# Two more key blocks per head on VectorE, one piece of the output projection loaded otherwise, and fewer semaphore waits, in a one-token attention and MLP kernel

## The chip, the cores and the metric

The kernel runs on one core of a Trainium2 chip. The metric is device time in microseconds (us). The kernel before takes 198.02 us, the median of three runs (198.01 to 198.27). Engine names are those of the profile: PE is TensorE, PEld its weight loads, DVE is VectorE, ACT is ScalarE, POOL is GpSimd, SP is SyncE (which here only issues DMAs).

## The reference

One token `x` (512 numbers) goes through an attention block with a cache of 4096 keys and values for each of 32 heads, and through an MLP; a gate mixes both.

```
g = sigmoid(sum(x * gate_w))
q = (x @ wq) as 32 heads of 128                       # wq: 512 x 4096
scores = q . k * 128**-0.5 ;  p = softmax(scores)     # k: 32 x 4096 x 128
o = p @ v                                             # v: 32 x 4096 x 128
a = o.reshape(4096) @ wo                              # wo: 4096 x 512
b = relu(x @ w1 + b1)**2 @ w2 + b2                    # w1: 512 x 1376, w2: 1376 x 512
out = g * a + (1 - g) * b
```

All tensors are bf16. Keys and values are 1 MB per head each, so 64 MB of the 78.76 MB that the kernel moves; wq and wo are 4 MB each.

## The kernel before

**Loads.** SP's queue first issues wq in four parts, then for each head one load of the keys (`load_k`) and one of the values (`load_v`), the keys seven heads ahead (`LAG = 7`). Each of keys and values has a ring of eight buffers. `load_k(h)` waits until head `h - 8` has been scored and transposed (`s_sd`, `s_t`), `load_v(h)` until the product with the values of head `h - 8` is done (`s_pv`). w1 is inserted at head 8. The last loads behind the last head's values are, in order: 8 of wo's 32 row groups (heads 24 to 31, `wob_sb`, into key buffer 0), eight tenths of w2 (`w2a`), the 128 rows of wo of head 23 (`wox`, into key buffer 1), the last 96 rows of w2 (`w2b`), and the last two tenths of w2.

**Pieces of wo.** The rows of wo of heads 0 to 22 are loaded as 92 pieces. A piece is 32 rows, 32 KB, and goes to one partition of tile `W`, over the space of wq, when all queries have been computed. The lists `RUNS` and `FIRST` (lines 59 to 65) say which partitions the pieces go to: an entry names a kind of place, a DMA engine `e`, and a number of pieces `k`, for engines `e`, `e + 1` and so on. `RUNS` are 14 DMAs from POOL's queue (lines 307 to 320), with 9 small DMAs between them that only advance the position from which engines are dealt out; `FIRST` are 5 DMAs that SP issues at heads 20 to 24 (lines 275 to 278). POOL then builds a selection matrix with one instruction for each of the 19 entries (lines 330 to 335).

**Scores.** A head has 32 blocks of 128 keys. The first `XB = 16` are scored on VectorE: `ttr(h)` does one multiply-and-sum instruction for each block against a broadcast query, in place on the key tile (line 629). The other `YB = 16` are transposed on TensorE in two halves (`transposes`, line 427), copied from PSUM by ScalarE (`evac`, line 361) and multiplied with the query column (`scores`, line 438). `smax(h)` on VectorE copies TensorE's scores beside its own and takes a maximum per partition (lines 635, 638). Every four heads (`G = 4`) share one maximum: `max_rows`, `gmax`, `max_cols`; ScalarE then computes the four exponentials (`exps`), and `pv(h)` on TensorE multiplies with the values (line 463).

**Order.** Every engine runs a hand-written loop over `i` from 0 to 38. At step `i` VectorE does `ttr(i)`, then `smax(i - 1)`; TensorE does `transposes(i)`, `scores(i - 1)`, and `pv(i - 7)` at the end of the step. At `i = 24` TensorE has the first MLP layer (`mlp_h`); at `i = 25` VectorE follows with `mlp` (lines 661 to 671) and POOL with a memset and its selection matrices.

**The end.** After `ttr(31)` VectorE normalises heads 16 to 23 (`norm(2)`, line 656). TensorE turns the result (`turn_a`, `spread_a`), VectorE copies it (lines 699 to 704), waits for all pieces of wo, and multiplies nine of the 32 row groups of the loaded pieces itself in `part_y` (lines 676, 679; `TD = 23`). TensorE does the other 23 in `out_a`, and adds VectorE's sum in `sum_y` (line 537), which stands ahead of `pv(30)` and `pv(31)` in its order. Then come `norm(3)`, `regroup`, `out_b` (line 525, heads 24 to 31), `mlp_out(0)`, `out_x` (line 531, head 23), `mlp_out(1)`, `mlp_out(2)` (line 546), the final add and transpose on VectorE (lines 717, 719), and the store.

## Time and profile before

| what | value |
|---|---|
| median of 3 runs | 198.02 us (198.01 to 198.27) |
| the profiled execution | 198.08 us, of which the span from first to last instruction is 196.3 us |
| DMA | 78.76 MB, mean 401 GB/s |
| PE busy | 132.9 us (68%) |
| PEld busy | 118.8 us (61%) |
| DVE busy | 139.5 us (71%) |
| ACT busy | 79.5 us (41%) |
| POOL busy | 29.9 us (15%) |

The 1.78 us between the profiled execution's time and its span lie around the span. In a group of instructions, the first number after the bar is the time in which at least one of them ran, then the mean of one in ns, then the idle time of the engine just before them and what ended it. In a table by stretches, each engine has its busy time and, in brackets, how many instructions ran; behind them stand the clock granted to TensorE, the share in which the DMA engines were busy, and what they moved in GB/s. In a timeline, a row is a run of equal instructions: start, length, engine, line, operation, tiles, count, and in square brackets the idle time before it and who ended it.

### The profile page before, as it was taken

Reading aid. Unit: us, or ns where it says so; the run is one execution under the profiler, and the core shown is the slowest. Engines: PE = TensorE matmul, PEld = TensorE weight load, DVE = VectorE, ACT = ScalarE, POOL = GpSimd, SP = SyncE. Lnnn points to the kernel's source line nnn. Section 1 sums busy time; section 2 is a strip of 40 time slices with the busy share of each in tenths; the row PEclk is TensorE's granted clock in tenths of the full one; section 3 lists DMA queues with packets and bytes.
Section 4 is the critical chain, followed back from the end, with each engine's and each line's share of the span. In section 5 each row is a group of like instructions: output and inputs, shape, how many; then the busy total and the mean of one; then the engine's idle time right before and its main releaser. Section 6 shows DMA issues by size and latency. Waiting matters only on the chain.

```text
span 196.3 us, 6564 instructions
## 1 busy us (share of the span) xinstructions
PE 132.9 (68%) x2402; PEld 118.8 (61%) x2408; DVE 139.5 (71%) x1152; ACT 79.5 (41%) x148; POOL 29.9 (15%) x53
## 2 busy tenths in 40 slices
PE   0128756699876867806697760769998677785872
PEld 0105725578675667706676760668997666785862
DVE  0307999999998687707877871777779999949310
ACT  2105838356473536503356330633077334611000
POOL 2000000000000000000019940000099750000000
PEclk9999978555585555665555555555555555555555
DMA  6999999999999999999999999999999999999990
GB/s 226 425 427 426 416 416 426 419 422 416 411 422 422 412 417 407 423 421 417 421 416 421 416 414 409 409 409 414 413 416 416 426 412 422 419 417 414 416 351 28
DMA packets 12730, 78.76 MB, mean 401 GB/s; under 512 B 2502, under 2 KB 2728, under 8 KB 3369
## 3 DMA queue, kind: packets, MB, share of 16 engines
q1 hardware_dynamic: 11146, 75.77, 93.6%
q0 software_dynamic: 1536, 2.56, 3.5%
q8 instruction: 19, 0.31, 0.6%
q14 instruction: 15, 0.11, 0.2%
q10 hardware_dynamic: 14, 0.01, 0.0%
HBM read 78.32 MB, written 0.00 MB: 399 GB/s over the span
## 4 chain that ended last, share of the span: by engine, by line
DMA 59%; DVE 22%; PE 9%; SPq 6%; issue 3%; ACT 0%
DMA Kt<-in_A_k_cache_dram 42%; DVE Kt L629 18%; DMA w2a<-in_B_w_dram 12%; DMA W<-in_A_wq_dram 6%; SPq L265 4%; PE KP L427 3%; PE pX L481 2%; DVE S L629 1%; SPq L260 1%; PE pQ L405 1%; PE pX L477 1%; PE pX L546 1%; SPq L254 1%; PE pS L438 1%; DVE dg L644 0%
## 5 line engine op out<-in xcount | busy, mean ns | idle before, releaser
L629 DVE CUSTOM_DVE_ANT_0 Kt<-Kt,qb 128x128 bf16<-128x128 bf16 x512 | 113.3, 289 | 23.2 <-DMA Kt<-in_A_k_cache_dram 23.2
L361 ACT ACTIVATE kT<-KP 128x1024 bf16<-128x1024 bf16 x64 | 61.8, 1021 | 68.8 <-PE KP L427 68.8
L427 PE MATMUL KP<-ident,Kt 128*128 128x128 bf16 x512 | 56.8, 300 | 32.8 <-DMA Kt<-in_A_k_cache_dram 32.8
L427 PEld LDWEIGHTS KP<-ident,Kt 128*128 128x128 bf16 x512 | 49.5, 140 | 35.6 <-DMA Kt<-in_A_k_cache_dram 34.4
L629 DVE DVE_READ_ACCUMULATOR2_ANT S<- 128x1 f32 x512 | 41.0, 80 | 0.0
L438 PEld LDWEIGHTS pS<-qcol,kT 128*128 128x128 bf16 x512 | 18.5, 107 | 10.7 <-DVE S L635 10.5
L438 PE MATMUL pS<-qcol,kT 128*128 128x1 bf16 x512 | 19.1, 167 | 8.4 <-DVE S L635 8.2
L315 POOL DMA_DIRECT2D xb<-in_B_w_dram x9 | 5.3, 590 | 100.3 <-PE pQ L405 100.3
L405 PE MATMUL pQ<-W,xb 128*128 128x512 bf16 x26 | 12.4, 620 | 7.8 <-DMA W<-in_A_wq_dram 6.4
L463 PEld LDWEIGHTS pO<-E,Vt 128*128 128x128 bf16 x512 | 15.5, 104 | 1.1 <-issue 0.8
L463 PE MATMUL pO<-E,Vt 128*128 128x1 bf16 x512 | 16.1, 165 | 0.0
L333 POOL TENSOR_SCALAR_AFFINE_SELECT w_sb<-w_sb 24x36 bf16<-24x36 bf16 (+5 forms) x19 | 11.0, 578 | 2.7
L353 ACT ACTIVATE qb<-pQ 128x512 bf16<-128x512 f32 x8 | 4.7, 591 | 14.9 <-PE pQ L405 14.9
L405 PEld LDWEIGHTS pQ<-W,xb 128*128 128x128 bf16 x32 | 3.6, 130 | 10.8 <-issue 10.8
L372 ACT ACTIVATE E<-S,nM 128x32 bf16<-128x32 f32 x32 | 9.9, 309 | 0.3
L463 PE MATMUL pQ<-E,Vt 128*128 128x1 bf16 x256 | 8.1, 165 | 2.3 <-DMA Vt<-in_A_v_cache_dram 2.0
L463 PEld LDWEIGHTS pQ<-E,Vt 128*128 128x128 bf16 x256 | 7.7, 104 | 2.5 <-issue 2.4
L463 PEld LDWEIGHTS pX<-E,Vt 128*128 128x128 bf16 x256 | 7.7, 103 | 0.5 <-issue 0.2
L463 PE MATMUL pX<-E,Vt 128*128 128x1 bf16 x256 | 8.0, 165 | 0.0
L318 POOL DMA_DIRECT2D W<-in_A_wo_dram x14 | 7.8, 563 | 0.0
L615 DVE CAST qcol<-pQ 128x4 bf16<-128x4 f32 x8 | 1.2, 152 | 8.4 <-PE pQ L413 8.4
L635 DVE COPY S<-pS 128x16 f32<-128x16 f32 x32 | 5.4, 168 | 2.2 <-PE pS L438 2.2
(84 smaller groups left out, 93.0 us busy)
## 6 DMA issues: line engine op xcount, KB each, us to landing
Kt<-in_A_k_cache_dram SPq DMA_DIRECT2D x32, 1024.0 KB, 27.2
Vt<-in_A_v_cache_dram SPq DMA_DIRECT2D x32, 1024.0 KB, 27.2
W<-in_A_wq_dram SPq DMA_DIRECT2D x4, 1024.0 KB, 7.9
W<-in_A_wo_dram POOLq DMA_DIRECT2D x2, 768.0 KB, 12.8
w_sb<-in_B_w_dram SPq DMA_DIRECT2D x4, 344.0 KB, 22.9
Kt<-in_A_wo_dram SPq DMA_DIRECT2D x1, 1024.0 KB, 21.5
w2a<-in_B_w_dram SPq DMA_DIRECT2D x1, 1024.0 KB, 23.3
W<-in_A_wo_dram POOLq DMA_DIRECT2D x10, 64.0 KB, 23.5
```

What stands on the lines that cost most here:

```text
L265: eng.dma_start(Vt[:, h % NV, :], v_h[h, :, :]).then_inc(s_v[h % NV], 16)
L315: eng.dma_start(dm[0:d, sent, :, 0:8], src[:, :, 0:8]).then_inc(s_dm[sent], 16)
L318: eng.dma_start(W[p:p + st * (k - 1) + 1:st, :], woa_v[q:q + k, :], max_dma_last_dim=8192).then_inc(s_wp[n], 16)
L333: eng.affine_select(out=part, in_=part, compare_op=ALU.not_equal, fill=1.0, base=-st * q, pattern=[[st, 4], [-1, st * (k - 1) + 1]], chann ...
L361: eng.activation(kT[:, h % 2, j * HB * 128:(j + 1) * HB * 128], KP[n % 3][:, :], ACT.Copy).then_inc(s_ev, 1)
L372: eng.activation(E[:, h % NE, :], S[:, h % NS, :], ACT.Exp, bias=nM[:, h:h + 1], scale=SCALE, accum_out=RS[:, h:h + 1]).then_inc(s_e, 1)
L405: mm = eng.matmul(pQ[:, :], xb[:, t, :], wq_sb[:, t, c * 512:(c + 1) * 512], start=(t == 0), stop=(t == 3))
L427: mm = eng.transpose(KP[n % 3][:, y * 128:(y + 1) * 128], Kt[:, h % NK, b * 128:(b + 1) * 128], ident[:, :])
L438: mm = eng.matmul(S2[:, y:y + 1], kT[:, h % 2, y * 128:(y + 1) * 128], qcol[:, h:h + 1], start=True, stop=True)
L463: mm = eng.matmul(O(h, h + 1), Vt[:, h % NV, b * 128:(b + 1) * 128], E[:, h % NE, b:b + 1], start=(b == 0), stop=(b == NB - 1))
L629: ins = eng.tensor_tensor_reduce(kb, kb, qb[:, h * 128:(h + 1) * 128], 1.0, 0.0, ALU.mult, ALU.add, S[:, h % NS, b:b + 1])
L635: eng.tensor_copy(S[:, h % NS, XB:NB], S2).then_inc(s_cp, 1)
```

## The change

- `XB` is 18: VectorE scores 18 of 32 blocks per head, TensorE transposes and multiplies 14 (two halves of 7).
- `RUNS` loses the entry with engines 3 and 4 (two pieces, POOL's queue). The last entry of `FIRST` has three pieces instead of two, on engines 0, 1 and 2. Pieces per engine, engines 0 to 15: before 8 7 6 1 6 5 5 8 8 5 5 5 5 5 5 8, after 8 7 7 0 5 5 5 8 8 5 5 5 5 5 5 8. 91 pieces are left.
- The 32 rows of the piece that fell out (the first 32 dimensions of head 22) are loaded as 32 rows of 1 KB into partitions 0 to 31 (`woy`), with one more DMA from SP behind `wox`; `out_x` has four more matmuls for them, and waits for both loads. The piece's number (`QX`) is skipped in the selection matrix.
- The pieces of POOL's queue count on one semaphore instead of 14, so TensorE and VectorE wait once where they had 14 waits each.
- Waits are left out or joined: `transposes` waits for ScalarE only in its second half from the third half on; `scores` waits for the query column and `ttr` for the broadcast query only at every fourth head; `pv` and `ttr` wait for the exponentials once for a group of four (for the group's last) instead of at every head.

```
-    XB = 16
+    XB = 18
...
-            (SEAM, 7, 2, 1, 1), (WRAP, 15, 2, 1, 1), (OUTER, 1, 2, 1, 1), (OUTER, 3, 2, 1, 1),
+            (SEAM, 7, 2, 1, 1), (WRAP, 15, 2, 1, 1), (OUTER, 1, 2, 1, 1),
...
-             (OUTER, 0, 2, 0, 1)]
+             (OUTER, 0, 3, 0, 1)]
+    QX = 4 * (NA - 2)
...
         for run in RUNS + FIRST:
+            q += q == QX
             yield (*place(*run), q)
...
+        woy = Kt[0:32, 1, DM:2 * DM]
...
-        s_wp = [sem(f"s_wp{n}") for n in range(len(RUNS))]
+        s_wp = sem("s_wp")
...
             eng.dma_start(wox, A_wo[HX * 128:NA * 128, :]).then_inc(s_wx, 16)
+            eng.dma_start(woy, A_wo[32 * QX:32 * QX + 32, :]).then_inc(s_wx, 16)
...
-                    if n >= 3:
+                    if n >= 3 and j == 1:
                         eng.wait_ge(s_ev, n - 2)
...
-                eng.wait_ge(s_qc, h // 4 + 1)
+                if h % 4 == 0:
+                    eng.wait_ge(s_qc, h // 4 + 1)
...
             def pv(h):
-                eng.wait_ge(s_e, h + 1)
+                if h % G == 0:
+                    eng.wait_ge(s_e, h + G)
...
                     eng.wait_ge(s_ac, 2)
-                    for q in s_wp:
-                        eng.wait_ge(q, 16)
+                    eng.wait_ge(s_wp, 16 * len(RUNS))
...
             def out_x():
-                eng.wait_ge(s_wx, 16)
-                for j in range(4):
-                    eng.matmul(acc[:, j:j + 1], wox[:, j * 128:(j + 1) * 128], onorm[:, HX:HX + 1],
-                               start=False, stop=False, skip_group_check=True)
+                eng.wait_ge(s_wx, 32)
+                for w, o in ((wox, onorm[:, HX:HX + 1]), (woy, onorm[0:32, HX - 1:HX])):
+                    for j in range(4):
+                        eng.matmul(acc[:, j:j + 1], w[:, j * 128:(j + 1) * 128], o,
+                                   start=False, stop=False, skip_group_check=True)
...
                 eng.wait_ge(s_k[h % NK], 16 * (h // NK + 1))
-                eng.wait_ge(s_qb, h // 4 + 1)
-                if h >= NS:
-                    eng.wait_ge(s_e, h - NS + 1)
+                if h % 4 == 0:
+                    eng.wait_ge(s_qb, h // 4 + 1)
+                if h >= NS and h % G == 0:
+                    eng.wait_ge(s_e, h - NS + G)
...
                     eng.tensor_copy(o2D, O2A[:, TD:32]).then_inc(s_y2, 1)
-                    for q in s_wp:
-                        eng.wait_ge(q, 16)
+                    eng.wait_ge(s_wp, 16 * len(RUNS))
                     eng.wait_ge(s_wr, 16 * len(FIRST))
                     eng.wait_ge(s_y2, 1)
                     part_y()
```

More of the change, by code (lines that the diff above doesn't have):

```diff
@@ L318, in _ @@
                 eng.dma_start(W[p:p + st * (k - 1) + 1:st, :], woa_v[q:q + k, :],
-                              max_dma_last_dim=8192).then_inc(s_wp[n], 16)
+                              max_dma_last_dim=8192).then_inc(s_wp, 16)
                 q += k
-            assert q == STRIPS[len(RUNS)][3] and STRIPS[-1][3] + STRIPS[-1][2] == 4 * HX
+            assert q == STRIPS[len(RUNS)][3] and STRIPS[-1][3] == QX + 1 and STRIPS[-1][2] == 3
             for n in range(sent):
```

## The prediction

> **What bounds the kernel now.** First the page's slices: the loads run at their full rate from the second slice to the last but two.

> ```profile
> DMA  6999999999999999999999999999999999999990
> GB/s 226 425 427 426 416 416 426 419 422 416 411 422 422 412 417 407 423 421 417 421 416 421 416 414 409 409 409 414 413 416 416 426 412 422 419 417 414 416 351 28
> PEclk9999978555585555665555555555555555555555
> ```

> So time can be won only where the loads end, and lost where work after the last landing grows. The chain of waits, cut to the end, shows who closes the kernel.

> ```profile
> 168.74 23.26 DMA w2a<-in_B_w_dram
> ...
> 192.14 0.99 PE pX L546 x32
> 193.13 0.11 PE pX L531 x4
> 193.23 0.35 PE pX L546 x12
> ```

> A load does. Next the timelines of TensorE and VectorE, to see how far behind the load the other claimants stand.

> ```profile
> 172.28 0.22 DVE L656 SCALAR_TENSOR_TENSOR onorm<-pO,gcol,rden 128x8 bf16<-128x8 f32 x1
> 176.37 0.49 DVE L676 TENSOR_SCALAR kT<-W,S 128x512 f32<-128x512 bf16 x1 [0.85 <-DVE S L704]
> 176.89 6.26 DVE L679 SCALAR_TENSOR_TENSOR kT<-W,S,kT 128x512 f32<-128x512 bf16 x8
> 183.21 1.01 PE L537 MATMUL pX<-onesf,kT 128*128 128x1 f32 x4 [0.43 <-DVE kT L679]
> 186.96 0.99 PE L463 MATMUL pQ<-E,Vt 128*128 128x1 bf16 x32
> 190.63 0.69 PE L525 MATMUL pX<-o2B,Kt 128*128 128x1 bf16 x20 [0.38 <-issue]
> 192.14 0.99 PE L546 MATMUL pX<-hs,w2a 128*128 128x1 bf16 x32 [0.82 <-DMA w2a<-in_B_w_dram]
> ```

> This is a second chain, only 0.82 us shorter: VectorE ends part_y at 183.15, TensorE waits for it, then runs from 183.21 without a gap to pv(31), and on through norm, regroup and out_b to 191.32. Last, where VectorE has room: stretches that each begin with ttr(26), (27), ... (31).

> ```profile
> 147.19:150.93 3.74, 2.96 (x53) 2.61 (x53) 3.71 (x35) 2.78 (x12) 3.65 (x1) 0.50 1.02 418
> 150.93:155.77 4.84, 3.33 (x69) 2.98 (x68) 4.81 (x36) 1.82 (x3) 3.57 (x9) 0.50 1.02 425
> 155.77:160.70 4.93, 3.82 (x73) 3.47 (x72) 4.90 (x36) 1.92 (x4) 3.64 (x10) 0.50 1.00 410
> 160.70:164.82 4.12, 2.71 (x60) 2.62 (x58) 4.05 (x38) 1.08 (x3) 0.13 (x1) 0.50 1.02 422
> 164.82:168.57 3.75, 2.54 (x57) 2.43 (x56) 3.72 (x35) 3.21 (x11) 0.00 (x0) 0.50 1.03 422
> 168.57:172.28 3.71, 3.17 (x66) 3.09 (x67) 3.68 (x35) 1.94 (x2) 0.00 (x0) 0.50 1.00 417
> ```

> The third busy time is VectorE's: in 25.09 us it is idle 0.24. Whatever is added to these six heads arrives whole at part_y.

> **VectorE's two blocks.** ttr(26) starts at 147.19 and its 16 blocks end with the copy at 150.59: 3.40 / 16 = 0.2125 us per block, 0.425 per head. Heads 0 to 25: 26 x 0.425 = 11.1 us, hidden, because VectorE sat 23.2 us waiting for keys (the group of line 629). Its first idle is at 62 us, so until then key buffers come free up to about 13 x 0.425 = 5.5 us later; a load takes 27.2 us (median) from issue to landing, nearly all of it in the queue, so SP may be that late. Without this cover it would cost one to one. Heads 26 to 31 have no cover: 6 x 0.425 = +2.55.

> Heads 27 and 28 took 4.84 and 4.93 instead of 3.74 while POOL ran its selection instructions. If each added block is stretched like its neighbours, 4 x 1.1 / 16 = +0.27; if the stall belongs to POOL's instructions, of which there is one less (18 of 19; 2.2 / 19), -0.1. I take -0.1, since the first of these heads, beside one long POOL instruction, took 3.74 like the heads without POOL: the stall goes with the count of instructions. [...]

> **TensorE's and ScalarE's relief.** Two of 16 transposes (1.89 / 16 each) and of 16 score matmuls (0.42 / 16) fewer: 0.24 + 0.05 per head. Mostly this lies in TensorE's waits for keys (32.8 us) and ScalarE's for TensorE (68.8), so nothing. It counts once: from the keys of head 24 at 132.91 TensorE runs without a gap through mlp_h to 141.35; POOL's memset (142.31) and its first selection (145.11) start from that, and hold VectorE until 147.19. Up to mlp_h that is one head's transposes and scores: -0.26 (bounds 0, if POOL's start doesn't follow, and -0.55, if the second head's counted too).

> **Waits.** Before part_y VectorE passes 16 waits in the 0.85 us shown above; 3 stay. Other dependent pairs on VectorE stand 0.04 apart (168.39 to 168.43), so 0.81 can go at most; 13/16 is 0.69. I take -0.70 (bounds -0.5, -0.81). TensorE's 13 lie behind a matmul (175.06 to 175.62): nothing. The waits joined by fours: pv(28) waits for its group's last exponential, 177.1 before and 178.6 to 179.3 then, and started at 178.63; pv(29) waits for its values until 181.78, which hides it. ttr and scores wait for results some 8 heads old: nothing.

> **Pieces and loads.** Bytes are equal. POOL's queue has one 0.55 us issue less (13; the 9 small ones stay, with 45 rows for 43) and nobody waits for its end. SP issues woy in about 0.45, ahead of w2b and w2a's tail, which land 22.8 and 21.5 us after issue: hidden. The third FIRST piece adds nothing to SP. In out_x 4 matmuls more: +0.11 by the chain. Which engine ends last changes: 32 KB at 26.1 GB/s (418 / 16) is 1.26 us on one engine. TensorE's program shrinks by some 340 instructions, so the 0.38 "issue" gap may sit elsewhere: +/-0.38.

> **Sum.** part_y ends 2.55 - 0.10 - 0.26 - 0.70 = 1.49 us later; TensorE's gapless run carries that to out_b, 191.32 + 1.49 = 192.81. The load's 0.82 is covered first: 1.49 - 0.82 + 0.11 = +0.78. The w2a tail (193.20) is then no longer waited for. 198.08 + 0.78 = 198.86; the profiled execution lies 0.06 above the median, so against that 198.80.

> **Rivals.**
> (a) Faster: the load still closes the kernel, and ends earlier. These stretches show it running out of engines:

> ```profile
> 191.00:191.50 0.50, 0.32 (x12) 0.23 (x9) 0.00 (x0) 0.00 (x0) 0.00 (x0) 0.50 0.41 148
> 191.50:192.00 0.50, 0.00 (x0) 0.00 (x0) 0.00 (x0) 0.00 (x0) 0.00 (x0) 0.50 0.36 131
> 192.00:192.50 0.50, 0.36 (x14) 0.39 (x15) 0.00 (x0) 0.00 (x0) 0.00 (x0) 0.50 0.19 72
> 192.50:193.00 0.50, 0.50 (x25) 0.50 (x23) 0.00 (x0) 0.00 (x0) 0.00 (x0) 0.50 0.02 8
> ```

> Shares times 16: six engines after 191.5, three after 192, none after about 192.7. If the last two are engines 3 and 4, each with a piece less, the end moves to the next ones, about 192.25: -0.45, 197.6. It decides only if VectorE's delay stays below about 0.35 instead of 1.49, for instance if the keys of head 24 come a us earlier; their arrivals were 4.93 to 5.60 apart, so they do wander. Against it: six heads without idle time.
> (b) No change: delay and slack cancel (delay near 0.8) and the loads end where they did: 198.0.
> (c) Slower through the loads: engine 2's extra piece, 1.26, makes it last: 199.3. Against: only a share of 0.41 is busy at 191.0 to 191.5, so 9 engines could take a piece unseen. [...]

> **Chances.** My forecast 0.63, (c) 0.07, (a) 0.18, (b) 0.12. Its own range is 198.1 (gap gone, keys earlier) to 199.6 (stretched blocks +0.37, relief absent +0.26). With the others, 197.5 to 199.7 leaves out two in ten. The measurement tells about 0.2% (0.4 us) from no change: slower 0.68 (most of the forecast, and (c)), the same 0.14, faster 0.18.

> **What would show it.** Right: ttr heads in 147 to 175 at 4.17 without POOL; part_y starting less than 0.3 after its copy and ending near 184.6; the idle time before mlp_out(0) gone, out_b's end near 192.8. Wrong: part_y ending before 184.0, or TensorE still waiting for w2a at the end.

## The result, and the profile after

The changed kernel takes 199.3 us (median of 12 runs, 198.4 to 199.5), the kernel before 198.09 us (12 runs on the same chips, 198.0 to 198.35). The ratio is 1.0054, with a 95% interval of 1.0045 to 1.0063: slower by about 1.1 us. The forecast was 198.8 (197.5 to 199.7). The profiled execution took 199.33 us with a span of 197.5, against 198.08 and 196.3.

The page's slices of the changed kernel, what the DMA engines moved in each:

```profile
GB/s 226 426 427 427 418 417 422 417 425 417 420 415 417 422 418 403 422 422 425 413 422 415 417 415 410 414 407 410 418 418 417 420 420 415 420 422 420 414 261 4
```

The loads run as before, and the slice that was half filled holds less (261 GB/s in the last but one, 351 before; a slice is 4.9 us): the work behind the loads has grown. The chain of waits of the changed kernel, its last part, start and length of each step:

```profile
174.32 0.53 PE pS L443 x14
...
184.55 1.01 PE pX L543 x4
...
191.28 1.01 PE pX L530 x32
192.56 0.73 issue
193.29 0.75 PE pX L552 x22
194.34 0.43 PE pX L552 x12
```

The load of `w2a`, which closed the kernel before, is gone from the chain. In its place stand a copy of VectorE's that TensorE waits for (174.32), `sum_y` (184.55), `out_b` (191.28), and 0.73 us in which TensorE has nothing to wait for and doesn't run. The timelines of VectorE and of TensorE show the same steps (start, length, engine, line, operation, tiles, count, idle time before and its end):

```profile
174.40 0.22 DVE L663 SCALAR_TENSOR_TENSOR onorm<-pO,gcol,rden 128x8 bf16<-128x8 f32 x1
177.71 0.49 DVE L683 TENSOR_SCALAR kT<-W,S 128x512 f32<-128x512 bf16 x1
```

```profile
174.32 0.53 PE L443 MATMUL pS<-qcol,kT 128*128 128x1 bf16 x14 [2.74 <-DVE S L642]
180.45 0.51 PE L512 MATMUL pX<-o2A,W 128*128 128x1 bf16 x14 [0.93 <-issue]
184.55 1.01 PE L543 MATMUL pX<-onesf,kT 128*128 128x1 f32 x4 [1.45 <-DVE kT L686]
191.28 1.01 PE L530 MATMUL pX<-o2B,Kt 128*128 128x1 bf16 x32 [0.26 <-DVE o2B L720]
192.16 0.41 PE L552 MATMUL pX<-hs,w2a 128*128 128x1 bf16 x10
193.29 0.75 PE L552 MATMUL pX<-hs,w2a 128*128 128x1 bf16 x22 [0.73 <-issue]
193.90 0.44 PE L537 MATMUL pX<-onorm,Kt 128*128 128x1 bf16 x8
```

VectorE's `norm(2)` comes at 174.40 (before 172.28), the wait ahead of `part_y` is gone, and `sum_y` starts at 184.55 (183.21). The "issue" gap in `out_b` is gone too; a larger one lies in `mlp_out(0)`, and another at 180.45, ahead of a wait that hides it. Last, the stretches between VectorE's copies of TensorE's scores (from the start of `ttr(26)` to the copy, then from copy to copy; columns as in the prediction):

```profile
146.69:150.51 3.82, 2.09 (x30) 1.74 (x27) 3.82 (x38) 2.29 (x10) 3.75 (x1) 0.50 1.01 412
150.51:156.37 5.86, 3.06 (x60) 2.72 (x60) 5.83 (x39) 2.28 (x3) 4.50 (x10) 0.50 1.02 425
156.37:161.22 4.85, 3.33 (x62) 3.07 (x62) 4.82 (x39) 1.73 (x2) 2.94 (x8) 0.50 1.00 412
161.22:165.42 4.20, 3.30 (x61) 2.90 (x61) 4.17 (x42) 1.18 (x2) 0.00 (x0) 0.50 1.02 423
165.42:169.98 4.56, 3.73 (x62) 3.28 (x62) 4.49 (x41) 2.83 (x11) 0.00 (x0) 0.50 1.01 417
169.98:174.09 4.11, 1.39 (x46) 1.30 (x46) 4.08 (x39) 0.94 (x2) 0.00 (x0) 0.50 1.01 421
```

Cut at the same events the kernel before has 3.40, 4.83, 4.87, 3.77, 4.16 and 3.76. VectorE is still never idle (0.21 of 27.40 us), and the six stretches are 2.61 us longer together, the three without GpSimd 0.43, 0.40 and 0.35.

### The profile page after: what moved, and what is told of

Its sections match the earlier page's. It is cut to its first block, busy times and chain, and to the rows that moved or that the text cites. A ratio compares the mean times of both kernels' runs of the same rounds, so it can differ in the third digit from the quotient of the medians.

```text
span 197.5 us, 6356 instructions
## 1 busy us (share of the span) xinstructions
PE 128.5 (65%) x2284; PEld 111.3 (56%) x2284; DVE 152.7 (77%) x1280; ACT 72.9 (37%) x148; POOL 29.7 (15%) x51
## 4 chain that ended last, share of the span: by engine, by line
DVE 46%; DMA 32%; PE 14%; SPq 4%; issue 2%; ACT 0%; DVEq 0%
DVE Kt L636 35%; DMA Kt<-in_A_k_cache_dram 27%; DMA W<-in_A_wq_dram 6%; DVE kT L686 3%; DVE S L636 2%; SPq L268 2%; PE pX L487 2%; PE pQ L409 2%; PE pQ L469 2%; PE KP L431 2%; DVE mp L645 1%; DVE hs L673 1%; SPq L263 1%; PE pX L543 1%; DVE S L642 1%
## 5 line engine op out<-in xcount | busy, mean ns | idle before, releaser
L636 DVE CUSTOM_DVE_ANT_0 Kt<-Kt,qb 128x128 bf16<-128x128 bf16 x576 | 127.0, 288 | 14.3 <-DMA Kt<-in_A_k_cache_dram 14.3
L365 ACT ACTIVATE kT<-KP 128x896 bf16<-128x896 bf16 x64 | 55.1, 914 | 69.6 <-PE KP L431 69.6
L431 PE MATMUL KP<-ident,Kt 128*128 128x128 bf16 x448 | 51.5, 304 | 26.9 <-DMA Kt<-in_A_k_cache_dram 26.8
L431 PEld LDWEIGHTS KP<-ident,Kt 128*128 128x128 bf16 x448 | 44.2, 142 | 29.3 <-DMA Kt<-in_A_k_cache_dram 28.1
L636 DVE DVE_READ_ACCUMULATOR2_ANT S<- 128x1 f32 x576 | 45.7, 79 | 0.0
L443 PE MATMUL pS<-qcol,kT 128*128 128x1 bf16 x448 | 17.3, 167 | 21.8 <-DVE S L642 21.8
L443 PEld LDWEIGHTS pS<-qcol,kT 128*128 128x128 bf16 x448 | 16.2, 107 | 25.8 <-DVE S L642 25.8
L409 PE MATMUL pQ<-W,xb 128*128 128x512 bf16 x32 | 15.0, 623 | 6.2 <-DMA W<-in_A_wq_dram 6.2
L322 POOL DMA_DIRECT2D W<-in_A_wo_dram x13 | 7.3, 565 | 0.0
L645 DVE TENSOR_REDUCE mp<-S 128x1 f32<-128x32 f32 x32 | 5.9, 185 | 1.1
## 6 DMA issues: line engine op xcount, KB each, us to landing
w_sb<-in_B_w_dram SPq DMA_DIRECT2D x4, 344.0 KB, 22.8
w2a<-in_B_w_dram SPq DMA_DIRECT2D x1, 1024.0 KB, 22.8
```

The source lines that it names most:

```text
L322: eng.dma_start(W[p:p + st * (k - 1) + 1:st, :], woa_v[q:q + k, :], max_dma_last_dim=8192).then_inc(s_wp, 16)
L365: eng.activation(kT[:, h % 2, j * HB * 128:(j + 1) * HB * 128], KP[n % 3][:, :], ACT.Copy).then_inc(s_ev, 1)
L409: mm = eng.matmul(pQ[:, :], xb[:, t, :], wq_sb[:, t, c * 512:(c + 1) * 512], start=(t == 0), stop=(t == 3))
L431: mm = eng.transpose(KP[n % 3][:, y * 128:(y + 1) * 128], Kt[:, h % NK, b * 128:(b + 1) * 128], ident[:, :])
L443: mm = eng.matmul(S2[:, y:y + 1], kT[:, h % 2, y * 128:(y + 1) * 128], qcol[:, h:h + 1], start=True, stop=True)
L636: ins = eng.tensor_tensor_reduce(kb, kb, qb[:, h * 128:(h + 1) * 128], 1.0, 0.0, ALU.mult, ALU.add, S[:, h % NS, b:b + 1])
```

## The experiments

Three theories stood against each other. Theory 1: VectorE's two blocks, late at `part_y`. Rival 1: the pieces, that is, the loads. Rival 2: TensorE's "issue" gaps, that is, the supply of its instructions. Ratios are against runs of the kernel before on the same chip, with 95% intervals; "gap" is idle time of TensorE that the profile calls "issue".

| run | median us | ratio |
|---|---|---|
| e1, blocks only | 200.04 | 1.0093 (1.0078 to 1.0108) |
| e2, all but the blocks | 198.24 | 1.0005 (0.9995 to 1.0014) |
| e3, pieces only | 198.18 | 1.0005 (0.9996 to 1.0014) |
| e4, waits only | 197.87 | 0.9984 (0.9974 to 0.9993) |
| e5, six row groups on VectorE | 199.68 | 1.0068 (1.0049 to 1.0087) |
| e6, 384 waits in front | 198.45 | 1.0016 (1.0006 to 1.0025) |
| e7, 13 waits before `part_y` | 199.27 | 1.0058 (1.0036 to 1.0079) |
| e8, selection matrix built early | 197.97 | 0.9992 (0.9983 to 1.0002) |
| e9, 128 waits in front | 198.2 | 1.0006 (0.9997 to 1.0016) |
| e10, 512 waits in front | 199.33 | 1.006 (1.0043 to 1.0076) |
| e11, e5 and e6 together | 198.89 | 1.0042 (1.0027 to 1.0057) |
| e12, 20 blocks | 200.45 | 1.0134 (1.0099 to 1.0168) |

### The parts of the change, each alone

**e1: the kernel before with only the blocks changed.**

```diff
-    XB = 16
+    XB = 18
```

> The kernel before with 18 blocks on VectorE and nothing else of the change. Theory (VectorE's chain: the six heads without idle time delay part_y, and TensorE's gapless run behind it closes the kernel instead of the load): norm(2) about 2.1 us later, the 0.85 us of waits before part_y still there, so sum_y starts near 185.3; 2.1 less the 0.82 of slack gives +1.3 us, 199.4, plus or minus 0.4 for where TensorE's issue gap falls. Rival 1 (the moved pieces and the extra load make the last load later): no effect here, 198.1. Rival 2 (TensorE's program has another length, and its issue gap in the last 10 us is what costs): at most +/-0.4 us, 197.7 to 198.5, with part_y no reason.

Measured: 200.04 us. Timelines of VectorE and TensorE of e1:

```profile
175.95 0.22 DVE L656 SCALAR_TENSOR_TENSOR onorm<-pO,gcol,rden 128x8 bf16<-128x8 f32 x1
```

```profile
186.82 1.01 PE L537 MATMUL pX<-onesf,kT 128*128 128x1 f32 x4 [3.17 <-DVE kT L679]
193.38 1.01 PE L525 MATMUL pX<-o2B,Kt 128*128 128x1 bf16 x32 [0.26 <-DVE o2B L714]
```

The blocks alone cost more than the whole change, and 0.24 more than the upper end of the expectation (199.8). `norm(2)` is 3.67 later than before; 1.13 of this is that GpSimd's memset, behind which VectorE's full stretch starts, began at 143.44 (142.31 before), and the other 2.54 is the forecast's 6 x 0.425; the expectation had no such late start. There is no gap in the tail (from `scores(31)` on): this run is VectorE's chain and nothing else.

**e2: the changed kernel with 16 blocks.**

```diff
-    XB = 18
+    XB = 16
```

> The changed kernel with 16 blocks on VectorE: the pieces, the extra load and the joined waits stay. Theory (VectorE's chain): part_y ends 0.7 us earlier than in the kernel before, about 182.4, the load closes the kernel again, 197.8 to 198.3. Rival 1 (pieces and loads): the slowdown stays whole, 199.2. Rival 2 (issue gap): the gap of 0.4 to 0.7 us that stands in mlp_out behind the last load stays, 198.5 to 198.8.

Measured: 198.24 us, no difference from before that the interval shows. Timeline of TensorE of e2:

```profile
177.99 0.51 PE L512 MATMUL pX<-o2A,W 128*128 128x1 bf16 x14 [0.75 <-issue]
180.81 1.02 PE L469 MATMUL pQ<-E,Vt 128*128 128x1 bf16 x32 [0.98 <-DMA Vt<-in_A_v_cache_dram]
191.65 0.99 PE L552 MATMUL pX<-hs,w2a 128*128 128x1 bf16 x32 [1.46 <-DMA w2a<-in_B_w_dram]
```

The load closes the kernel again, with 1.46 us to spare for VectorE's chain. A gap of 0.75 is there, but TensorE waits for values and for `w2a` behind it, so it costs nothing. All of the slowdown needs the blocks.

**e3: the kernel before with only the pieces changed** (`RUNS`, `FIRST`, `QX`, `woy` and the four matmuls, as in the diff of the change).

> The kernel before with the changed pieces, the 32 rows as a load of their own and their four matmuls, 16 blocks, all waits. Theory (VectorE's chain): part_y where it was, 183.15 +/- 0.5; the load closes the kernel, 198.0 to 198.3 (four matmuls 0.1 more). Rival 1 (pieces and loads): 199.2. Rival 2 (issue gap): 198.1, since TensorE's program is as long as before up to its last 20 matmuls.

Measured: 198.18 us, ratio 1.0005: nothing, so rival 1 falls. `mlp_out(0)` waits 1.00 us for `w2a`, until 191.97.

**e4: the kernel before with only the waits joined or left out.**

> The kernel before with only the waits joined or left out (one semaphore for the pieces of the POOL queue). Theory (VectorE's chain): the gap before part_y shrinks from 0.85 to about 0.14 and part_y ends near 182.4, but the load closes the kernel, so 198.1 and the idle time of TensorE before mlp_out(0) grows from 0.8 to about 1.5. Rival 1 (pieces and loads): 198.1. Rival 2 (issue gap): TensorE has some 90 instructions less in front, the gap moves from out_b, where the wait for the load hides it, into mlp_out, where nothing does: +0.4 to +0.7, 198.5 to 198.8.

Measured: 197.87 us, faster by 0.16%, the lowest ratio of all kernels here. The profiled execution, 198.02, is not one of the faster ones, so what makes them faster is not shown. TensorE's timeline of e4:

```profile
178.35 0.51 PE L508 MATMUL pX<-o2A,W 128*128 128x1 bf16 x14 [0.96 <-issue]
192.08 0.99 PE L547 MATMUL pX<-hs,w2a 128*128 128x1 bf16 x32 [1.49 <-DMA w2a<-in_B_w_dram]
```

The gap has moved from `out_b` to 178.35, where the load's slack hides it. Rival 2's cost does not occur where a load closes the kernel. Over e2 to e4, `w2a` is there at 191.65 and 191.97 with the new pieces and at 192.08 without (192.14 before).

### Is it `part_y`, or TensorE's instructions?

The changed kernel's end (TensorE's last matmul 194.75, before 193.57) is 1.18 later, but `mlp_out(0)` starts 0.02 later than before. The rest comes after it. So the next runs ease or tighten `part_y`, and shift TensorE's instructions.

**e5: part of `part_y` given to TensorE** (26 of the 32 row groups there, 6 on VectorE).

```diff
-    TD = 23
+    TD = 26
...
+                if i == 38:
+                    out_a(6)
```

> The changed kernel with part_y shortened: VectorE multiplies 6 of the 32 row groups of wo instead of 9 (three instructions of 0.78 less, -2.35 us), TensorE 26 instead of 23 (12 matmuls, +0.3). Theory (VectorE's chain): part_y ends near 182.3 instead of 184.49, TensorE waits for w2a again, and the load closes the kernel: 198.0 to 198.4, about 1 us faster than the changed kernel. Rival 1 (pieces and loads): stays at 199.2. Rival 2 (TensorE's issue gap): 199.2, or less by the gap at most.

Measured: 199.68 us, not faster than the changed kernel. Theory 1 alone fails here. Timeline of TensorE of e5:

```profile
180.04 0.51 PE L512 MATMUL pX<-o2A,W 128*128 128x1 bf16 x14 [0.73 <-issue]
182.55 0.99 PE L543 MATMUL pX<-onesf,kT 128*128 128x1 f32 x4
186.34 0.69 PE L469 MATMUL pQ<-E,Vt 128*128 128x1 bf16 x20 [1.62 <-issue]
192.63 0.19 PE L530 MATMUL pX<-o2B,Kt 128*128 128x1 bf16 x2 [0.48 <-issue]
```

`sum_y` runs at 182.55 without any wait, 2.0 us earlier, and TensorE loses nearly all of it to gaps of 1.62 and 0.48: its last matmul ends at 194.46, 0.29 before that of the changed kernel. (The profiled execution is the fastest of the four, 199.05.) Something else limits TensorE at almost the same place.

**e6: the changed kernel with 384 waits, already fulfilled, in TensorE's first 24 steps.** They compile to 192 instructions in TensorE's program, not to the 384 of the expectation: its trace has 253 semaphore instructions there, the changed kernel's 61. The two gaps that the expectation puts one page apart are 512 instructions apart in the changed kernel's trace, two pages as counted below.

```diff
+                if i < 24:
+                    for _ in range(16):
+                        eng.wait_ge(s_cst, 1)
```

> The changed kernel with 16 more waits, on a semaphore that is long set, in each of TensorE's first 24 steps: 384 instructions more in front of the end, so the issue gap (0.93 at 179.5 and 0.73 at 192.56, one page of the program apart) falls elsewhere in it. Theory (VectorE's chain): sum_y starts at 184.5 as in the changed kernel, and the 0.73 in mlp_out falls before it or away: 198.5 +/- 0.3. Rival 2 (the gap is not tied to the place in the program): it stays, 199.2. If the waits themselves hold TensorE up, its steps before 100 us grow, where it waits for keys or for VectorE.

Measured: 198.45 us, 0.85 below the changed kernel, by instructions that do nothing. Timeline of TensorE of e6:

```profile
181.33 0.54 PE L469 MATMUL pQ<-E,Vt 128*128 128x1 bf16 x14 [0.84 <-issue]
184.66 1.02 PE L543 MATMUL pX<-onesf,kT 128*128 128x1 f32 x4 [1.52 <-DVE kT L689]
191.22 1.01 PE L530 MATMUL pX<-o2B,Kt 128*128 128x1 bf16 x32 [0.26 <-DVE o2B L723]
192.10 0.99 PE L552 MATMUL pX<-hs,w2a 128*128 128x1 bf16 x32
```

VectorE is as late as in the changed kernel (`sum_y` at 184.66), but from there to the end no gap is left. An earlier start of GpSimd is not the reason: its memset began at 141.90, in the changed kernel at 141.80. The gap at 181.33 is the one that stood at 180.45, 32 matmuls further on in the program (there 2 matmuls into a group of `out_a`, here 18 into the `pv` behind it).

**e7: the changed kernel with 13 waits put back before `part_y`.**

```diff
                     eng.wait_ge(s_wp, 16 * len(RUNS))
+                    for _ in range(13):
+                        eng.wait_ge(s_wp, 16 * len(RUNS))
```

> The changed kernel with 13 waits more on VectorE in front of part_y, all long satisfied. Theory (VectorE's chain): the gap before part_y grows from 0.14 to 0.8 or 0.85, part_y ends 0.7 later, and as nothing behind it has slack the kernel takes 0.7 more, 199.9. Rival 1 (loads close the kernel): no effect, 199.2.

Measured: 199.27 us, no change: a miss for theory 1, which had 199.9. Thirteen waits on one semaphore made the idle time before `part_y` 0.50 us where it had been 0.14, so the dose was half of what was meant; `sum_y` came 0.28 later, at 184.83. But the gap in `mlp_out(0)` shrank from 0.73 to 0.17 at the same time: the matmul behind it starts at 192.84 instead of 193.29, although all before it was later. In these two profiles the gap's end isn't tied to `part_y`.

**e8: the changed kernel with the selection matrix in a tile of its own, built in the first 12 us.**

```diff
-        selA = w1_sb[0:NA, 2, 0:512].rearrange("h (c p) -> h c p", c=4)
+        selA_sb = sb("selA", [NA, 512], bf16)
+        selA = selA_sb[:, :].rearrange("h (c p) -> h c p", c=4)
...
+            eng.memset(selA_sb[:, :], 0.0).then_inc(s_sa, 1)
...
-                eng.wait_ge(s_sb, 2 + len(STRIPS))
+                eng.wait_ge(s_sa, 1 + len(STRIPS))
+                eng.wait_ge(s_sb, 2)
```

> The changed kernel with the selection matrix of the pieces in a tile of its own, built by GpSimd in its first 15 us instead of from 147 to 161. Theory (VectorE's chain): heads 27 and 28 lose their stalls (5.8 and 4.9 us between copies become 4.2), norm(2) comes about 2 us earlier, part_y ends near 182.5, and the load closes the kernel: 198.0 to 198.4. If the stalls don't come from GpSimd's instructions: 199.2. Rival 1 (pieces and loads): 199.2.

Measured: 197.97 us, level with the kernel before. VectorE's stretches 27 and 28, 5.86 and 4.85 in the changed kernel, are 4.11 and 4.19. Timelines of VectorE and TensorE of e8:

```profile
172.42 0.22 DVE L667 SCALAR_TENSOR_TENSOR onorm<-pO,gcol,rden 128x8 bf16<-128x8 f32 x1
```

```profile
178.54 0.53 PE L516 MATMUL pX<-o2A,W 128*128 128x1 bf16 x14 [1.00 <-issue]
182.57 1.02 PE L547 MATMUL pX<-onesf,kT 128*128 128x1 f32 x4 [0.75 <-DVE kT L690]
191.78 0.99 PE L556 MATMUL pX<-hs,w2a 128*128 128x1 bf16 x32 [1.40 <-DMA w2a<-in_B_w_dram]
```

With 1.98 us taken from VectorE's lateness the load closes the kernel again, gap or not. So without VectorE's lateness there is no slowdown, the gaps' part included.

### Where the borders of TensorE's instruction pages fall

The trace shows TensorE's program arriving in packets of a queue of its own: 19 in the kernel before, 18 after, 0.29 MB, so 16 KB each. The packets fit pages of 256 instructions. In the changed kernel's trace TensorE runs 256 (matmuls, weight loads and semaphore instructions) from where it resumes at 180.45 to where it resumes at 186.75, and 256 again to 193.29. The 2284 matmuls, 2284 weight loads and 61 semaphore instructions of the changed kernel's trace make 18.1 of them, and in all fourteen traces, from 4373 instructions (17 packets) to 4945 (19), the number of packets is the whole part of that quotient. Every gap in the tail ends about the same time after such a packet starts (a packet takes 0.95 to 1.17 us in the changed kernel; starts from the trace's DMA records):

| kernel | packet starts at | TensorE resumes at | between |
|---|---|---|---|
| before | 188.07 | 190.63 | 2.56 |
| changed | 177.96, 184.36, 190.68 | 180.45, 186.75, 193.29 | 2.49, 2.39, 2.61 |
| e5 | 177.71, 183.81, 189.96 | 180.04, 186.34, 192.63 | 2.33, 2.53, 2.67 |
| e7 | 177.91, 190.27 | 180.26, 192.84 | 2.35, 2.57 |

**e9: 128 waits (64 instructions) in front.**

```diff
+                if i < 16:
+                    for _ in range(8):
+                        eng.wait_ge(s_cst, 1)
```

> The changed kernel with 128 waits (they compile to 64 instructions) added in TensorE's first 16 steps, long before the stretch at the end; nothing is left out. TensorE's program then crosses each page of 256 instructions 64 instructions earlier. Supply theory (a page's fetch starts when TensorE crosses into the page before it, and a page takes 6.2 to 6.4 us while the loads run): the crossing that came just after the stall at scores(31), 174.3, comes before that stall; the fetch then starts some 2 us earlier, the gap of 0.73 in mlp_out is gone or at most 0.3, and the time is 198.6 +/- 0.3. If a gap of fixed size only moves with the page's border: 0.7 us idle some 30 to 60 matmuls earlier in out_b or mlp_out, and 199.2 as the changed kernel. If GpSimd's start sets all of it and the pages nothing: 199.2.

Measured: 198.2 us (197.92 to 198.25), no longer to be told from the kernel before. Timeline of TensorE of e9:

```profile
173.95 0.53 PE L443 MATMUL pS<-qcol,kT 128*128 128x1 bf16 x14 [2.74 <-DVE S L645]
184.18 1.01 PE L543 MATMUL pX<-onesf,kT 128*128 128x1 f32 x4 [2.48 <-DVE kT L689]
191.71 0.99 PE L552 MATMUL pX<-hs,w2a 128*128 128x1 bf16 x32
```

The packets start at 174.17, 181.02 and 187.45, over 3 us earlier than in the changed kernel, and no gap is left in the tail. The wait at `scores(31)` is the same 2.74. The time is 0.1 below the lower end of the supply theory's range. `sum_y` is 0.37 earlier, as GpSimd's memset began 0.36 earlier in this profile, so not all of the 1.1 us between e9 and the changed kernel need come from the pages; e6, with a later start, has 0.85 of it.

**e10: 512 waits in front, the control.** They were meant to be 256 instructions, one page; the trace has 264 more than the changed kernel's (325 semaphore instructions for 61), a page and 8.

```diff
+                if i < 24:
+                    for _ in range(22 if i < 8 else 21):
+                        eng.wait_ge(s_cst, 1)
```

> The changed kernel with 512 waits (256 instructions, one whole page) added in TensorE's first 24 steps; nothing is left out. A control: the borders of the pages fall on the same instructions again. Supply theory: the gaps lie where they lay in the changed kernel (out_a, pv(30), mlp_out near 193.3, 0.6 to 0.8 us), 199.2 +/- 0.3. If the added waits themselves make the time shorter, not the borders: 198.4 as with the 384 waits.

Measured: 199.33 us, the changed kernel's time again. Timeline of TensorE of e10:

```profile
180.90 0.19 PE L469 MATMUL pQ<-E,Vt 128*128 128x1 bf16 x2 [1.20 <-issue]
187.19 0.80 PE L469 MATMUL pQ<-E,Vt 128*128 128x1 bf16 x24 [0.28 <-issue]
193.19 0.85 PE L552 MATMUL pX<-hs,w2a 128*128 128x1 bf16 x26 [0.19 <-issue]
```

Four times the waits of e9, and none of the gain. The gaps are back, each four matmuls earlier in the program than in the changed kernel (26 matmuls of `mlp_out(0)` stand behind the last, 22 there), 2.52 to 2.57 us after the packets at 178.38, 184.62 and 190.66; 19 packets are in the trace for 18. Four matmuls with their weight loads are the 8 instructions by which the added ones exceed a page. In e6 the 192 added ones are 64 short of a page, and its gap came 32 matmuls later. It is the borders, not the waits. The gaps' sizes differ (0.28 and 0.19 for the last two), which the expectation had not; TensorE's end, 194.75, is the same. From start to start the gaps cost 0.44 in `pv(30)` and 0.35 in `mlp_out(0)`, and `sum_y` is 0.28 later: 1.07 together. In the changed kernel the two cost 0.18 and 0.89: 1.07. This fits pages that set the end, with `sum_y`'s delay only filling what TensorE would have waited anyway.

**e11: e5 and e6 together.**

> The changed kernel with part_y's row groups moved, 6 on VectorE and 26 on TensorE, and with the 384 waits (192 instructions) in TensorE's first 24 steps; nothing is left out. VectorE then ends part_y near 181.9, before TensorE asks for sum_y. If part_y and the instruction pages are two limits side by side, and both are eased here: no wait at sum_y, no gap over 0.3 after 186, 198.0 to 198.3, closed by the load again. If the pages still bind, as 3 more matmul groups stand in the stretch: a gap of 0.3 to 0.8 after 186 and 198.4 to 198.8. If part_y never mattered: 198.45 as with the 384 waits alone.

Measured: 198.89 us, 0.09 above the range for pages that still bind. Timeline of TensorE of e11:

```profile
181.23 0.53 PE L469 MATMUL pQ<-E,Vt 128*128 128x1 bf16 x14 [0.80 <-issue]
182.90 0.99 PE L543 MATMUL pX<-onesf,kT 128*128 128x1 f32 x4
187.43 0.59 PE L512 MATMUL pX<-o2A,W 128*128 128x1 bf16 x16 [0.76 <-issue]
193.35 0.21 PE L552 MATMUL pX<-hs,w2a 128*128 128x1 bf16 x2 [0.74 <-issue]
```

`sum_y` waits for nothing, and TensorE still ends at the pages' pace: packets at 178.79, 184.84 and 190.74, resuming 2.44, 2.59 and 2.61 later. In this order of the work the pages alone hold the kernel 0.8 us above the kernel before, whatever VectorE does after 174.

**e12: 20 blocks.**

```diff
-    XB = 18
+    XB = 20
```

> The changed kernel with 20 of 32 key blocks on VectorE instead of 18; nothing is left out. Theory 1 (each added block costs 0.2125 us in each of the six last heads, uncovered): norm(2) 2.3 to 2.6 later, near 176.8; sum_y near 187.0; 201.3 to 201.8. If TensorE's instruction pages and not VectorE set the end of the changed kernel: at most 0.5 more, 199.4 to 199.8. If GpSimd's start takes a part of it: 200.3 to 201.0.

Measured: 200.45 us. Timelines of VectorE and TensorE of e12:

```profile
176.72 0.22 DVE L663 SCALAR_TENSOR_TENSOR onorm<-pO,gcol,rden 128x8 bf16<-128x8 f32 x1
```

```profile
186.81 1.02 PE L543 MATMUL pX<-onesf,kT 128*128 128x1 f32 x4 [1.53 <-DVE kT L686]
194.33 0.99 PE L552 MATMUL pX<-hs,w2a 128*128 128x1 bf16 x32
```

Theory 1's steps come out: `norm(2)` at 176.72 for 176.8, `sum_y` at 186.81 for 187.0. Its time does not: 1.15 more than the changed kernel instead of 2.0 to 2.5. `mlp_out(0)` starts 2.17 later, but TensorE's program has changed its borders, the gap of the changed kernel in `mlp_out(0)` (0.89 from start to start) is gone, and 2.17 - 0.89 = 1.28, which is what TensorE ends later. The time lies in the range for a part taken by GpSimd's start (200.3 to 201.0), but that part is small: the memset began at 141.56, 0.24 earlier than in the changed kernel.

## Why the prediction was right, and where it was not

**Step by step.** Predicted, then measured in the changed kernel's profile:

| step | predicted | measured |
|---|---|---|
| six heads on VectorE | +2.55 | +2.61 with GpSimd's share |
| GpSimd's stalls | -0.10 (+0.27 left to the range) | +0.16 (heads 27 and 28 took 1.01 more, less 0.85) |
| GpSimd's start, from TensorE's relief | -0.26 | -0.50 |
| `norm(2)`, the sum of these | +2.19 | +2.12 |
| waits before `part_y` | -0.70 | -0.71 (0.85 to 0.14) |
| `sum_y` | +1.49 | +1.34 |
| start of `mlp_out(0)` | +0.67 | +0.02 |
| from there to `out_x` | 0 | +0.89 |
| `out_x` to the last matmul | +0.11 | +0.27 |
| TensorE's end | +0.78 | +1.18 |

The first part stands. VectorE is full from `ttr(26)` on and each block arrives at `part_y` (e1: 2.54, e12: 176.72 for 176.8); the heads without GpSimd took 0.35 to 0.43 more each, for 0.425. The waits before `part_y` went as worked out, for the other waits no cost shows (e4's gain of 0.16% stays unexplained), and the pieces were worth nothing (e3, 198.18), so rival (c) is gone. Which DMA engine a piece goes to, and that the small DMAs advance the dealing, is how the kernel's lists have it; no trace here names engines. What rival (a) forecast was there in part: `w2a` lands 0.17 (e3) and 0.49 us (e2) earlier with the new pieces, in single profiles. Its landing no longer decided anything. Stretches of the changed kernel at the end, the DMA share being the last but one number:

```profile
191.50:192.00 0.50, 0.50 (x25) 0.50 (x23) 0.00 (x0) 0.00 (x0) 0.00 (x0) 0.50 0.15 47
192.00:192.50 0.50, 0.50 (x21) 0.47 (x18) 0.00 (x0) 0.00 (x0) 0.00 (x0) 0.50 0.11 25
```

The shares after 191.5 are 0.15 and 0.11, where they had been 0.36 and 0.19.

Two of the first part's terms were off and cancelled: GpSimd's stalls grew a little although there was one selection less (nearer to the +0.27 that I had left to the range), and GpSimd's start came 0.50 earlier, not 0.26. The -0.26 is also a slip: its own terms, 0.24 + 0.05, make 0.29. GpSimd's start wandered between profiles by more than that (the memset began at 143.44 in e1, at 141.44 in e9); what sets it was not tried and stays open. That GpSimd's selections hold VectorE was shown by e8: without them two stretches fell from 10.71 to 8.30, 2.41 us for 18 selections. That their count alone sets the price, as the forecast's -0.10 had it, does not hold to a tenth: 19 selections had cost 2.18 (4.83 + 4.87 less twice 3.76), so 18 would cost 2.07. What in a selection holds VectorE was not shown.

**The step that was mis-sized** is the one on TensorE's program: "the 0.38 'issue' gap may sit elsewhere: +/-0.38". (That program is 309 instructions shorter by the traces, 4629 for 4938, not some 340.) I had put the gap in the range and not in the sum, and had carried `part_y`'s delay through a run "without a gap". Measured from start to start, the old gap had cost 0.55 and is gone. With 0.14 that the slack of 0.82 understated (the pipelined end of `out_b` overlaps the next start), 0.15 less delay at `sum_y`, and 0.18 for a new small gap in `pv(30)`, `mlp_out(0)` starts 0.65 earlier than forecast: -0.55 - 0.14 - 0.15 + 0.18 = -0.66. The new gap behind it costs 0.89, and the eight matmuls of `out_x` 0.16 more than the 0.11 put down for them. -0.66 + 0.89 + 0.16 = +0.39, against the +0.40 by which TensorE's end missed the forecast.

So the sign and nearly the size came out, but not all of it for the reason given. With the old gap out of the sum, the slack put right and no new gap, the forecast's own chain gives 0.78 - 0.55 - 0.14 = +0.09, no change that could be seen. That new gaps then fell into the tail and added as much as they did was luck. Of the signs named, the heads without GpSimd (4.20 and 4.11 us, and 4.56 where the step for the maxima falls), `part_y`'s start 0.14 after its copy, its end at 184.49 and the vanished wait for `w2a` came as described; the end of `out_b` did not (192.29 for 192.8). Where no gap falls behind `sum_y`, about the same VectorE delay makes 198.2 (e9) to 198.45 us (e6), 0.06% and 0.16% above the kernel before by their ratios: VectorE's delay by itself uses up the slack of the load and little more, near to rival (b). The other 0.85 to 1.1 us are the place of the page borders, with a TensorE that is held 2.74 us at `scores(31)` by VectorE's copy and has to run everything after it at full speed. Both need VectorE's lateness (e2, e8). The forecast's chain was one of two limits that stood within a few tenths of each other, and e5 and e11 show the other one alone.

**What stays open.** When exactly a page is asked for was not measured; that it hangs on an earlier crossing is argued from the packets' times and from e9 and e10. Why a page takes 6 us was not tried either, but the traces hold a hint. While the loads run, the next packet starts 3.3 to 3.9 us after TensorE has resumed (the changed kernel, e5, e7, e10, e11). After the last resume, at 192.6 to 193.3, it starts 1.1 to 1.3 us later (the changed kernel, e5, e7, e10), and by then the loads have run out (a DMA share of 0.11 at most from 192 on). So more than half of the time from resume to packet looks like waiting among the loads; no run tests it. e12's lower gain over theory 1 and e7's lack of an effect fit the borders, but only through single profiles.

## What to carry to other kernels

Here TensorE, held up late (2.74 us at `scores(31)`) and then run flat out, met its instruction supply as a limit of its own: look on such a kernel for "issue" gaps, and for packets of the instruction queue ahead of each gap's end (2.33 to 2.67 us ahead here). Before a change of 0.5% is believed or dismissed on such a kernel, shift the page borders with a few idle instructions far in front (64 of them came with 1.1 us less here, 192 with 0.85 less, 264, a page and 8, with nothing) and compare again. And a chain that ends 0.8 us before the closing load lands leaves little to spend on a full engine: two blocks per head, in six heads without cover, cost 2.5 us.

## What the runs showed of the hardware that I had not expected

TensorE's instructions came as pages of 256 (16 KB packets of 0.95 to 1.17 us in the changed kernel; 256 instructions lie between its gaps, and the count of packets fits in all fourteen traces); while the loads run, pages followed each other after 5.9 to 6.4 us where TensorE starved (the changed kernel, e5, e7, e10, e11), against the estimate of 3.4 us in which TensorE uses one up, and it stood idle for 0.17 to 1.62 us at a time. The tails of e1 and e9 have no gap; in e2 and e4 gaps of 0.75 and 0.96 us cost nothing, since TensorE waits for a load behind them; at the end of the changed kernel one of 0.73 us is followed by no wait, and cost 0.89 from start to start.

Waits on a semaphore that was already there cost no time in front: 384 made 192 instructions (e6), and 512 in TensorE's first 24 steps left the kernel's time where it was (e10, 199.33 for 199.3). What one costs where TensorE is busy was not measured. And 13 waits on one semaphore held VectorE for only 0.36 us, where 16 waits on different ones had taken 0.85 with the wait for the copy.
